# Filter turned in DRAM ahead of its stage, four staging places, and a new order of groups, closings and loads

## The chip, the cores and the metric

The kernel runs on one core of one Trainium2 chip. The metric is the device time of one execution in microseconds (us). Three executions of the kernel before took 1017.70, 1017.57 and 1022.55 us (median 1017.7). The profile comes from a further execution that took 1021.45 us; its span, from the first to the last instruction, is 1019.7 us, so 1.75 us lie around it.

## The reference, cut to what matters

S = 2048 rows, D = 576 columns, DFF = 4608, all float32.

```python
x  = A_q
xn = layernorm(x)
# A: short causal convolution of k (4 taps), times v, long causal convolution with ssm_k, gate
kv = sum(pad(k)[:, t:t + S] * shift_k[:, 3 - t] for t in range(4)) * v
y  = irfft(rfft(kv, 2 * S) * rfft(ssm_k.T, 2 * S))[:S] + kv * ssm_D      # per column, along S
A  = xn * y
# B: feed-forward
B  = relu(xn @ w1) @ w2                                                 # 576 -> 4608 -> 576
out = x + A + B
```

The filter `ssm_k` is stored as [D, S]: one row of 2048 values for each column d of the output.

## The kernel before, in words

Two things run interleaved, and TensorE (PE) works for both.

**The feed-forward** is the main line. It is cut into 36 steps ("quads"): two halves of the rows, each with 18 slices of 256 hidden units. The first three steps (`PLAIN`, up to about 95 us) use the plain product (`classical`), the other 33 a product with seven block products in place of eight (`quad`, L640). Weights and operands are split in a high and a low part, and three of the four part products are made. In a quad, PE makes the hidden values (`psh`, products of 512 columns) and between them eight "units" (`mm2`, L744) of the quad before: 12 products of 288 columns into one of two PSUM places (`pso`), whose sum VectorE (DVE) then adds to `acc` in SBUF (L772). A unit whose number is in `stage["seeded"]` goes another way: ScalarE (ACT) first copies `acc` into the PSUM place (L742), PE adds onto it, and ACT copies the result back to `acc` (L765); DVE has nothing to do for it. A quad's own DVE work is `sums` (L531), `u` (L697), `p` (L704), `ll` (L602); ACT makes the high parts (L518, L597), copies `psh` (L661, L699), and GpSimd (POOL) makes the low parts of the weights (L519) and issues the loads of the weights (`r<-in_w`, L500 to L511).

**The stream** `conv()` makes everything else and is a generator. `tick` (L1219) is called after each group of products with their column count; it pulls the next piece of the stream when its planned cost is covered. `yield` gives a cost, a negative number a pause in columns, and "wide" asks for a PSUM place borrowed from the units. `with here()` puts DVE and ACT instructions behind the feed-forward's last ones on the same engine. Each engine works its instructions in the order in which they were placed; a DMA has no such edge, and SP's queue is filled by the planner that lays out the program. The stages of the stream, with the times of the profiled execution, are:

1. `later_operands` (L401, 91 to 232 us). The second half of x is loaded (L408, `area<-in_x`), normalized, stored (`rows_n`, L428), loaded back in turned pieces (L444), transposed and combined into seven operands (L464). Each operand is split chunk by chunk, 14 chunks in all (n = 0 to 13): ACT makes the high part (L473) and DVE the low part (L474) in a staging place, and SP stores it (`ops<-area`, `ops_s<-area`, L476). There are three staging places, used in turn, so chunk n writes where chunk n - 3 was stored from.
2. The filter is loaded into `kt` by `load_filter` (L827): 16 DMAs of 288 KB, one for 36 columns d and one half of the SBUF partitions. With `d (p t) -> p d t`, t = 32, each piece of such a load is 32 values, 128 bytes. Eight of them are asked for beside the chunks from n = 6 on (L477), eight after them, each followed by a pause of `KT_GAP` = 6000 columns (L885 to L887).
3. The filter stage (L937 to L952, 262 to 338 us). 32 copies (L941, L943) bring `kt[:, :, t]` into order; 11 groups of products (`filter_group`, L903) each take up to 864 of 9216 columns, ACT and DVE copy the result from PSUM to `z` (L867, L869), and SP stores `z` to `zk` (L910), up to six stores a group. The last of the 11 groups is the short one (576 columns) and comes one copy after the tenth.
4. The input stage (338 to 650 us): taps, gate and products of k and v, stored to `zx`. Here units 3 and 4 of each quad are seeded (L955).
5. The middle stage (675 to 910 us): 18 pairs of chunks. For each, the filter's part is copied (L1044) and swapped (L1049), multiplied (L1074), swapped by four DMAs on SP (`area<-area`, L1079), joined by DVE (`join`, L1084), turned back on PE (`psg`/`psf`, L785) and stored to `zy`.
6. The output stage (910 to 999 us) loads `zy`, x and `fin` (L1150 to L1161), gates and adds.

`rate` (L1212) spreads the planned cost of the stream over the columns of the feed-forward that are left when all pauses are taken off.

Of the kernel before, what the change touches and what calls it, by code (L numbers as in the profile page):

```python
# [17 lines left out]
P = 128  # L18
# [18 lines left out]
A1 = 64  # L37
# [18 lines left out]
NCH = NG * D // CW  # L56
KG = 432
KD = 36
KT_GAP = 6000
N_FB, N_FS, N_FK, N_FX, N_FM, N_FO = 23, 14, A2, T * (2 * KS + 1) + 2, NCH // 2, T  # L60
W_FB, W_FS, W_FK, W_FX, W_FMK, W_FMX, W_FMB, W_FO = 2.6, 3.0, 1.9, 2.2, 4.0, 3.5, 2.9, 3.9
CONV_TOTAL = (N_FB * W_FB + N_FS * W_FS + N_FK * W_FK + N_FX * W_FX + N_FM * (W_FMK + W_FMX + W_FMB)
# [37 lines left out]
def h3_ffn_kernel(ctx: ExitStack, tc, x, k, v, shift_k, ssm_k, ssm_D, w1, w2, fwd, inv, mid, out):  # L100
# [26 lines left out]
    fin = dram.tile([HT // 2, P, 2, D], F32, name="fin")  # L127
    rows_n = dram.tile([HB, BT // 2, 2, P, D], F32, name="rows_n")
    ops_n = {o: dram.tile([P, 2, 2, 512], F32, name=f"ops_{o}") for o in OPERANDS}
    hl_n = dram.tile([HB, P, 512], F32, name="hl_n")  # L130
    scale_n = dram.tile([2 * BT, P], F32, name="scale_n")

# [27 lines left out]
    def halves(u):  # L160

        return slice(u * A1, (u + 1) * A1), slice((1 - u) * A1, (2 - u) * A1)

    def move(tile_, rows, t, store=False, queues=(nc.sync, nc.sync)):
        for u in range(U):
            a, b = tile_[halves(u)[0]], rows[u, :, t]
            queues[u].dma_start(*((b, a) if store else (a, b)))

    pairs = {}

# [146 lines left out]
    def spread_scales(pool):  # L317

        sq, turned = (pool.tile([P, 32], F32, tag=f"sq{n}", name=f"sq{n}") for n in range(2))
        nc.vector.tensor_copy(sq, rstd[:, :2 * BT].unsqueeze(1).to_broadcast([P, 4, 2 * BT]))  # L320
        nc.vector.transpose(turned, sq)
        for q in range(P // 32):
            queue = nc.scalar if q % 2 else nc.sync
            queue.dma_start(scale_n[:, 32 * q:32 * q + 32], turned[32 * q:32 * q + 2 * BT])
        for b in (1, 0):
            row[b] = pool.tile([P, 512], F32, tag=f"row{b}", name=f"row{b}")
            src = scale_n[b * BT:(b + 1) * BT].rearrange("(o i) p -> o (i p)", o=1)
            nc.sync.dma_start(row[b], src.to_broadcast([P, 512]))

    def scaled(o, b):  # L330
        if isinstance(o, int):
# [69 lines left out]
    def later_operands(view, views, load_filter):  # L401


        first = HB * BT
        rows = {}
        for t in range(first, T, 2):
            rows[t] = view((t - first) // 2 * 2 * D, 2, D)
            move(rows[t], x, slice(t, t + 2))  # L408
        yield -PAUSE
        for t0 in range(first, T, 4):  # L410
            for t in range(t0, t0 + 4):
                with here():
                    stats(t, rows[t - t % 2][:, t % 2, :])
                yield W_FB / 2
            shift = xp.tile([P, 4], F32, tag="shift", name=f"shift{t0}", bufs=2)
            with here():
                inv_std(t0, 4)
                nc.vector.scalar_tensor_tensor(shift, mv[:, t0:t0 + 4, 0], -1.0, rstd[:, t0:t0 + 4],
                                               op0=OP.mult, op1=OP.mult)
            yield W_FB / 2  # L420
            for t in range(t0, t0 + 4):
                pair = rows[t - t % 2]
                with here():
                    nc.scalar.activation(pair[:, t % 2, :], pair[:, t % 2, :], AF.Identity,
                                         scale=rstd[:, t:t + 1], bias=shift[:, t - t0:t - t0 + 1])
                yield W_FB / 2
                if t % 2:
                    nc.sync.dma_start(rows_n[t // BT - HB, t % BT // 2].rearrange("t p d -> p t d"),  # L428
                                      pair)
        order = [(b, c) for b in range(HB) for c in range(5)]  # L430
        yf = {f"{b}{k}": view(HB * BT * D + (2 * b + k) * 1024, 2, 512)
              for b in range(HB) for k in range(2)}
        for n, o in enumerate(("s1", "s2")):
            yf[o] = view(REST + 1024 * n, 2, 512)
        ws = {}

        def load(n):
            if n < len(order):
                b, c = order[n]
                src = rows_n[b].rearrange("h t (g p) d -> p (h t g) d", p=32)  # L440
                w = ws[n] = view(n % 4 * 512, 512)
                for i in range(4 if c < 4 else 2):
                    d = c * P + 32 * i
                    nc.sync.dma_start(w[32 * i:32 * i + 32].rearrange("p (g d) -> p g d", d=32),  # L444
                                      src[:, :, d:d + 32])

        for n in range(2):
            load(n)
        yield -PAUSE
        for n, (b, c) in enumerate(order):  # L450
            load(n + 2)
            with here():
                if c < 4:
                    nc.vector.transpose(yf[f"{b}{c // 2}"][:, c % 2, :], ws[n])
                else:
                    v, r = (view(2048 + (2 * b + k) * 512, 512) for k in range(2))
                    nc.vector.transpose(v[:64], ws[n][:64])
                    split_rest(r.bitcast(F32R), v)
                    nc.sync.dma_start(hl_n[b], r)
            yield W_FB  # L460
        n = 0
        stages_o = Ring(*views(REST + 2048, 2, 2, 512), view(3072, 2, 512))
        for o in ("00", "11", "s1", "s2", "01", "s3", "s4"):
            for c in range(2):  # L464
                with here():
                    combine(None, yf, (o,), c)
                if o[0] == "s":
                    yield W_FB / 2
                if n == HB * 3:
                    stages_o.views = (*stages_o.views[:2], yf["11"])  # L470
                dst = stages_o.put(n)
                with here():
                    nc.scalar.activation(dst[:, 0].bitcast(F32R), yf[o][:, c, :], AF.Copy)  # L473
                    nc.vector.tensor_tensor(dst[:, 1].bitcast(F32R), yf[o][:, c, :],  # L474
                                            dst[:, 0].bitcast(F32R), OP.subtract)
                nc.sync.dma_start(ops_n[o][:, :, c, :], dst)  # L476
                if n >= 6:  # L477
                    load_filter()
                n += 1
                yield W_FS  # L480
# [340 lines left out]
    def stages(view, views):  # L821


        kt = view(KT, NH, A2)
        blocks = [(d, h) for d in range(0, NH, KD) for h in range(2)]

        def load_filter():  # L827
            if blocks:
                d, h = blocks.pop(0)
                src = ssm_k[h * NH + d:h * NH + d + KD, :].rearrange("d (p t) -> p d t", t=A2)  # L830
                with here():
                    nc.sync.dma_start(kt[halves(h)[0], d:d + KD, :], src)

        z = view(Z, 2, 2 * CW)
        mats = Ring(*views(WT, 4, U, P))
# [62 lines left out]
                nc.vector.tensor_tensor(kt[row, :, 0], kt[row, :, 0], skip[row, :], OP.add)  # L898
        order = [T * u + t for t in range(T) for u in range(U)]
        flat = A2 * NH  # L900
        starts = list(range(0, flat, 2 * KG))

        def filter_group(a):  # L903
            parts = divided(a, min(a + 2 * KG, flat), KG, NH)
            group([[(w, lambda r, u=order[e] // T, t=order[e] % T: mats["k", t][:, u, :],
                     copies[e][:, c:c + w]) for e, c, w, _ in part] for part in parts],
                  KG, ("act", "dve"))
            for e, c, w, off in divided(a, min(a + 2 * KG, flat), flat, NH)[0]:
                for r in range(2):
                    nc.sync.dma_start(at_t(zk, order[e])[:, :, r * NH + c:r * NH + c + w],  # L910
                                      z[:, r, off:off + w])
# [25 lines left out]
        for e, t2 in enumerate(order):  # L937
            to = copies.put(e)
            with here():
                if e % 2:  # L940
                    nc.vector.tensor_copy(to, kt[:, :, t2])  # L941
                else:
                    nc.scalar.activation(to, kt[:, :, t2], AF.Copy)  # L943
            if e == A2 - 1:
                load(0)
            yield W_FK / 2
            while starts and min(starts[0] + 2 * KG, flat) <= e * NH + (e == A2 - 1) * NH:
                yield "wide"
                filter_group(starts.pop(0))
                yield W_FK / 2 / (len(range(0, flat, 2 * KG)) / A2)  # L950
            if e % U and e // U + 2 < T:
                load_mat(("k", e // U + 2), e // U + 2, nc.sync)  # L952


        stage["seeded"] = (3, 4)  # L955

        def tap(t, n):

# [110 lines left out]
        def multiplied(n, banks, filt):  # L1069

            for c in (1, 0):
# [4 lines left out]
                if c:  # L1076
                    for a in range(0, P, A2):
                        b = a ^ A2
                        nc.sync.dma_start(other[b:b + A2], filt[c][a:a + A2])  # L1079

        def join(n):
            to = parts[0][n]
# [98 lines left out]
                added.add(t)  # L1181

        for i in range(4):
            load_rest(i)
        for i in range(4):
            load_z(i)
        yield -1.75 * PAUSE
# [21 lines left out]

    stream = conv()  # L1210
    clock = {"ffn": 0.0, "conv": 0.0, "until": 1e9, "done": False, "wide": False}
    rate = CONV_TOTAL / (SHARE * FFN_TOTAL - PAUSES * PAUSE - 8 * KT_GAP)  # L1212

    def rest_of_stream():
        for _ in stream:
# [133 lines left out]
```

## Time and profile before

| | |
|---|---|
| three runs, median | 1017.70, 1017.57, 1022.55; 1017.7 us |
| profiled execution, its time | 1021.45 us |
| its span | 1019.7 us |
| granted PE clock over the span | 1.000 |
| PE, DVE, POOL, ACT busy | 99%, 68%, 45%, 43% of the span |

The profile names a group of instructions by line, engine and `out<-in`. A bracket such as `[2.19 <-ACT area L473]` is the idle time of the engine before the instruction, in us, and what ended it. `SPq` rows are DMA issues: the first number is when the issue began, the second how long SP was held; a DMA's landing is a different, later time. The view of waits has the total in us, the number of times, and the longest.

### The profile page before, as it was taken

What the parts mean: (1) busy time and instruction counts of PE and PEld (TensorE: products, weight loads), DVE (VectorE), ACT (ScalarE), POOL (GpSimd) and SP (SyncE); (2) the same over time, 40 slices, a digit from 0 to 9 for tenths busy, and PEclk for the clock granted to TensorE, in tenths of its full rate; (3) what the DMA queues carried; (4) which work ended last, traced back from release to release, by engine and by line L of the source; (5) the groups of instructions that cost most, each with busy time, mean ns of one, the idle gap of its engine ahead of it and who ended that gap; (6) DMA issues with size and microseconds to landing.
All of it is one profiled execution on the core that took longest, in us unless ns stands there. A gap on an engine that the chain in (4) does not pass through costs nothing.

```text
span 1019.7 us, 17381 instructions
## 1 busy us (share of the span) xinstructions
PE 1004.9 (99%) x6502; PEld 844.4 (83%) x6502; DVE 697.7 (68%) x1059; ACT 436.8 (43%) x765; POOL 460.5 (45%) x500
## 2 busy tenths in 40 slices
PE   9999999999999999999999999999999999999997
PEld 5998999889877898898889889887777777777787
DVE  6787677774665697787768768556667666666764
ACT  7244443443455244445354444544554544532220
POOL 4335444444443855645555454424533234434450
PEclk9999999999999999999999999999999999999999
DMA  6214389898465724359862433468889879878964
GB/s 172 90 50 113 102 186 193 186 224 137 135 204 183 214 76 129 93 167 376 255 193 89 136 107 91 153 184 241 247 242 262 269 230 276 222 220 240 277 183 116
DMA packets 129720, 185.22 MB, mean 182 GB/s; under 512 B 69042, under 2 KB 83508, under 8 KB 128740
## 3 DMA queue, kind: packets, MB, share of 16 engines
q1 hardware_dynamic: 113332, 130.82, 46.2%
q0 software_dynamic: 15952, 52.40, 17.4%
q8 instruction: 51, 0.84, 0.4%
q10 hardware_dynamic: 352, 0.89, 0.3%
q14 instruction: 33, 0.27, 0.1%
HBM read 119.57 MB, written 45.62 MB: 162 GB/s over the span
## 4 chain that ended last, share of the span: by engine, by line
PE 90%; DMA 4%; DVE 3%; issue 1%; ACT 1%; POOL 1%; SPq 0%; DVEq 0%; POOLq 0%; ACTq 0%
PE pso L575 42%; PE psh L575 34%; PE psg L785 5%; PE psf L785 4%; PE psh_c L575 3%; DMA ops_s<-area 1%; DMA r<-in_w 1%; DMA zk<-area 1%; PE psw L1260 1%; DVE ll L602 1%; DVE sums L531 0%; DVE x L297 0%; PE psx L235 0%; SPq L910 0%; POOL wd L519 0%
## 5 line engine op out<-in xcount | busy, mean ns | idle before, releaser
L575 PE MATMUL pso<-w,hh 128*128 128x288 f32 x2304 | 466.8, 296 | 1.0 <-DVE area L869 0.8
L575 PEld LDWEIGHTS pso<-w,hh 128*128 128x128 f32 x2304 | 378.0, 188 | 30.8 <-issue 7.6
L575 PE MATMUL pso<-w,ll 128*128 128x288 f32 x1152 | 339.5, 295 | 0.0
L772 DVE TENSOR_TENSOR acc<-pso,acc 128x576 f32<-128x576 f32 x240 | 180.4, 754 | 123.9 <-PE pso L575 123.3
L575 PEld LDWEIGHTS pso<-w,ll 128*128 128x128 f32 x1152 | 216.2, 188 | 0.0
L519 POOL TENSOR_TENSOR wb<-sums,wb 128x512 fp32r<-128x512 f32 x33 | 47.6, 1441 | 291.8 <-ACT wb L518 266.2
L519 POOL TENSOR_TENSOR w<-r,w 128x576 fp32r<-128x576 f32 x72 | 108.1, 1509 | 124.6 <-ACT w L518 124.4
L575 PE MATMUL psh<-x,wa 128*128 128x512 f32 x396 | 102.4, 394 | 3.3 <-DVE p L704 2.2
L575 PE MATMUL psh<-xs,wb 128*128 128x512 f32 x396 | 102.1, 393 | 0.0
L575 PEld LDWEIGHTS psh<-x,wa 128*128 128x128 f32 x396 | 72.4, 188 | 18.8 <-DVE p L704 2.7
L575 PE MATMUL psh<-hl,wr 128*128 128x512 f32 x264 | 85.3, 404 | 0.8 <-ACT psh L699 0.8
L602 DVE SCALAR_TENSOR_TENSOR ll<-psh,hh 128x512 fp32r<-128x512 f32 x66 | 45.3, 687 | 55.1 <-ACT hh L597 55.1
L519 POOL TENSOR_TENSOR wa<-r,wa 128x512 fp32r<-128x512 f32 x36 | 56.5, 1570 | 54.0 <-ACT wa L518 53.9
L575 PEld LDWEIGHTS psh<-xs,wb 128*128 128x128 f32 x396 | 70.8, 188 | 11.4
L699 ACT ACTIVATE psh<-psh 128x512 f32<-128x512 f32 x33 | 19.2, 582 | 117.4 <-DVE u L697 117.4
L785 PE MATMUL psg<-area 64*64 64x512 f32 (+10 forms) x632 | 64.2, 472 | 1.5 <-issue 1.5
L575 PEld LDWEIGHTS psh<-hl,wr 128*128 128x128 f32 x264 | 45.9, 188 | 21.6 <-issue 10.8
L597 ACT ACTIVATE hh<-psh 128x512 fp32r<-128x512 f32 x66 | 39.3, 595 | 47.6 <-PE psh L575 47.4
L597 ACT ACTIVATE hh<-p 128x512 fp32r<-128x512 f32 x33 | 20.9, 634 | 88.1 <-PE pso L575 43.4
L697 DVE TENSOR_TENSOR u<-psh,u 128x512 f32<-128x512 f32 x33 | 22.8, 691 | 45.3 <-PE psh L575 45.2
L785 PE MATMUL psf<-area 64*64 64x512 f32 (+10 forms) x528 | 51.1, 451 | 0.7 <-DVE area L941 0.7
L575 PE MATMUL psh<-xs,wc 128*128 128x512 f32 x198 | 51.2, 393 | 0.0
(137 smaller groups left out, 1498.9 us busy)
## 6 DMA issues: line engine op xcount, KB each, us to landing
r<-in_w POOLq DMA_DIRECT2D x70, 288.0 KB, 4.0
area<-area SPq DMA_DIRECT2D x144, 128.0 KB, 4.8
r<-in_w POOLq DMA_DIRECT2D x35, 512.0 KB, 4.9
zk<-area SPq DMA_DIRECT2D x64, 144.0 KB, 2.9
area<-zk SPq DMA_DIRECT2D x18, 512.0 KB, 4.3
area<-zx SPq DMA_DIRECT2D x18, 512.0 KB, 6.2
zy<-area SPq DMA_DIRECT2D x18, 512.0 KB, 3.1
area<-zy SPq DMA_DIRECT2D x32, 288.0 KB, 7.2
```

The costliest lines, as they stand in the source:

```text
L519: nc.gpsimd.tensor_tensor(w[:, 1, :n], src, w[:, 0, :n], OP.subtract)
L575: last = nc.tensor.matmul(ps, a, m, start=start and n == 0, stop=n == len(seq) - 1, skip_group_check=True)
L597: done["act"] = nc.scalar.activation(hh, ps, AF.Relu)
L602: done["ll"] = nc.vector.scalar_tensor_tensor(ll, ps, 0.0, hh, op0=OP.max, op1=OP.subtract)
L697: nc.vector.tensor_tensor(u2, x, u2, OP.add)
L699: nc.scalar.activation(x, y, AF.Copy, scale=-1.0)
L772: done["acc"] = nc.vector.tensor_tensor(two(acc[t]), ps[:, :, :NH], two(acc[t]), OP.add)
L785: done["pe"] = nc.tensor.matmul(ps, a, m, start=start, stop=stop, skip_group_check=True)
L1260: last = nc.tensor.matmul(idle[0], warm[:, :P], warm, start=True, stop=True)
```

## The change

- `relay_filter` is new. It copies `ssm_k` to a DRAM tensor `kt_n` [half, p, d, t] by 16 DRAM-to-DRAM DMAs, 288 KB each, with the same 128-byte pieces. Ten of them stand on SP behind the loads of the scales (`row`, L328, in `spread_scales`), six behind the loads of the second half of x.
- `load_filter` loads from `kt_n`: 8 DMAs of 576 KB on all 128 partitions, 4608 bytes in one piece for each partition. Four are asked for beside the chunks n = 6, 8, 10 and 12, four after them, each with a pause of 9000 columns. `rate` subtracts 4 x 9000 in place of 8 x 6000.
- The staging of the chunks has three places for n = 0 to 5 and four for n = 6 to 13 (the fourth is where operand "s1" was, no longer needed then).
- The 11 filter groups are cut so that the first is the one with 576 columns. A group is made as soon as its columns are copied, so the groups now follow copies 2, 5, 8, ..., 29 and 31 in place of 3, 6, ..., 30 and 31 (counted from 0).
- In the input stage units 3 and 7 are seeded in place of 3 and 4.
- At the start of the output stage the first four `load_rest` (x on SP, `inv` on POOL) have an edge behind the last swap of the middle stage (L1079).

```diff
-KT_GAP = 6000
+KT_GAP = 9000
+FIRST = 5 * KD
...
+    kt_n = dram.tile([U, A1, NH, A2], F32, name="kt_n")
...
+    def relay_filter(behind, part):
+        for d in range(*part, KD):
+            for h in range(U):
+                src = ssm_k[h * NH + d:h * NH + d + KD, :].rearrange("d (p t) -> p d t", t=A2)
+                with tc.issue_after(behind.ins):
+                    behind = nc.sync.dma_start(kt_n[h, :, d:d + KD, :], src)
...
-            nc.sync.dma_start(row[b], src.to_broadcast([P, 512]))
+            last = nc.sync.dma_start(row[b], src.to_broadcast([P, 512]))
+        relay_filter(last, (0, FIRST))
...
-            move(rows[t], x, slice(t, t + 2))
+            last = move(rows[t], x, slice(t, t + 2))
+        relay_filter(last, (FIRST, NH))
...
-        stages_o = Ring(*views(REST + 2048, 2, 2, 512), view(3072, 2, 512))
+        two_o = views(REST + 2048, 2, 2, 512)
+        stages_o = [*two_o, view(3072, 2, 512)] * 2 + [*two_o, yf["11"], yf["s1"]] * 2
...
-                if n == HB * 3:
-                    stages_o.views = (*stages_o.views[:2], yf["11"])
-                dst = stages_o.put(n)
+                dst = stages_o[n]
...
-                if n >= 6:
+                if n >= 6 and n % 2 == 0:
                     load_filter()
...
-        blocks = [(d, h) for d in range(0, NH, KD) for h in range(2)]
+        blocks = list(range(0, NH, KD))
...
-                d, h = blocks.pop(0)
-                src = ssm_k[h * NH + d:h * NH + d + KD, :].rearrange("d (p t) -> p d t", t=A2)
+                d = blocks.pop(0)
                 with here():
-                    nc.sync.dma_start(kt[halves(h)[0], d:d + KD, :], src)
+                    nc.sync.dma_start(kt[:, d:d + KD, :],
+                                      kt_n.rearrange("h p d t -> (h p) d t")[:, d:d + KD, :])
...
-        starts = list(range(0, flat, 2 * KG))
+        cuts = [0, *range(flat % (2 * KG), flat + 1, 2 * KG)]
+        spans = list(zip(cuts, cuts[1:]))
...
-            while starts and min(starts[0] + 2 * KG, flat) <= e * NH + (e == A2 - 1) * NH:
+            while spans and spans[0][1] <= e * NH + (e == A2 - 1) * NH:
                 yield "wide"
-                filter_group(starts.pop(0))
+                filter_group(*spans.pop(0))
...
-        stage["seeded"] = (3, 4)
+        stage["seeded"] = (3, 7)
...
-                        nc.sync.dma_start(other[b:b + A2], filt[c][a:a + A2])
+                        done["swap"] = nc.sync.dma_start(other[b:b + A2], filt[c][a:a + A2])
...
         for i in range(4):
-            load_rest(i)
+            with tc.issue_after(done["swap"].ins):
+                load_rest(i)
...
-    rate = CONV_TOTAL / (SHARE * FFN_TOTAL - PAUSES * PAUSE - 8 * KT_GAP)
+    rate = CONV_TOTAL / (SHARE * FFN_TOTAL - PAUSES * PAUSE - 4 * KT_GAP)
```

More of the change, by code (lines that the diff above doesn't have):

```diff
@@ L166, in move @@
             a, b = tile_[halves(u)[0]], rows[u, :, t]
-            queues[u].dma_start(*((b, a) if store else (a, b)))
+            last = queues[u].dma_start(*((b, a) if store else (a, b)))
+        return last
     pairs = {}
@@ L900, in stages, with filter_group @@
         flat = A2 * NH
-        starts = list(range(0, flat, 2 * KG))
-        def filter_group(a):
-            parts = divided(a, min(a + 2 * KG, flat), KG, NH)
+        cuts = [0, *range(flat % (2 * KG), flat + 1, 2 * KG)]
+        spans = list(zip(cuts, cuts[1:]))
+        def filter_group(a, b):
+            parts = divided(a, b, KG, NH)
             group([[(w, lambda r, u=order[e] // T, t=order[e] % T: mats["k", t][:, u, :],
@@ L907, in filter_group @@
                   KG, ("act", "dve"))
-            for e, c, w, off in divided(a, min(a + 2 * KG, flat), flat, NH)[0]:
+            for e, c, w, off in divided(a, b, flat, NH)[0]:
                 for r in range(2):
@@ L946, in stages @@
             yield W_FK / 2
-            while starts and min(starts[0] + 2 * KG, flat) <= e * NH + (e == A2 - 1) * NH:
+            while spans and spans[0][1] <= e * NH + (e == A2 - 1) * NH:
                 yield "wide"
-                filter_group(starts.pop(0))
-                yield W_FK / 2 / (len(range(0, flat, 2 * KG)) / A2)
+                filter_group(*spans.pop(0))
+                yield W_FK / 2 / ((len(cuts) - 1) / A2)
             if e % U and e // U + 2 < T:
                 load_mat(("k", e // U + 2), e // U + 2, nc.sync)
-        stage["seeded"] = (3, 4)
+        stage["seeded"] = (3, 7)
         def tap(t, n):
```

## The prediction

> **What bounds the kernel now.** I read the page's head first, then the waits of PE alone, then the chain that ended last, and then the timeline around each wait.
>
> ```profile
> span 1019.7 us, 17381 instructions
> PE 1004.9 (99%) x6502; PEld 844.4 (83%) x6502; DVE 697.7 (68%) x1059; ACT 436.8 (43%) x765; POOL 460.5 (45%) x500
> ```
>
> PE is busy for 1004.9 of 1019.7 us, and no other engine is near; the granted clock is 1.00 in every window below. The change neither removes nor adds a product, so all it can win is idle time of PE: 14.8 us. Part of that is the start and the last store. The view of PE's waits between 40 and 1000 us shows the rest (who waited for whom: us in total, times, longest):
>
> ```profile
> PE psh L575 <- DVE p L704: 2.2, 1, 2.2
> PE psg L785 <- issue: 1.5, 1, 1.5
> PE psh L575 <- ACT psh L661: 1.0, 1, 1.0
> PE pso L575 <- DVE area L869: 0.8, 1, 0.8
> PE psh L575 <- ACT psh L699: 0.8, 1, 0.8
> PE psf L785 <- DVE area L941: 0.7, 1, 0.7
> PE pso L575 <- DVE acc L772: 0.2, 1, 0.2
> ```
>
> These seven single waits add up to 7.2 us; that is the ceiling. Since ends of products are modelled, I check the largest pair by the distance of equal steps, in the chain (start, length, what):
>
> ```profile
> 143.80 3.23 PE psh L575 x14
> ...
> 168.06 3.23 PE psh L575 x14
> ...
> 193.76 7.79 DMA ops_s<-area
> ...
> 220.40 3.23 PE psh L575 x14
> ```
>
> A quad without stream products takes 168.06 - 143.80 = 24.26 us. From 168.06 to 220.40 stand two: 52.34 - 48.52 = 3.82 us lost, where the waits on L704 and L661 show 3.2. The chain says by what: stores of operand chunks.
>
> **The staging places.** Picked from the timelines of ACT, DVE and PE there (start, length, instruction, idle time before it and what ended it):
>
> ```profile
> 201.63 0.63 ACT L473 ACTIVATE area<-area 128x512 fp32r<-128x512 f32 x1 [2.66 <-DMA ops_s<-area]
> 202.30 0.69 DVE L474 TENSOR_TENSOR area<-area 128x512 fp32r<-128x512 f32 x1 [2.60 <-ACT area L473]
> 204.91 1.65 PE L575 MATMUL psh<-x,wa 128*128 128x512 f32 x6 [2.23 <-DVE p L704]
> 207.64 0.63 ACT L473 ACTIVATE area<-area 128x512 fp32r<-128x512 f32 x1 [0.92 <-DMA ops_s<-area]
> ```
>
> ACT stands 2.66 us because its staging place is still being stored. DVE works in order, so L704, which PE needs, stands behind L474. The store issued at 193.76 had landed only at 201.55. Why so late (a stretch with each engine's busy time, clock, DMA share and GB/s; the issues of the filter loads, ns, and their landing; the speed in 40 slices of 222 to 232 us):
>
> ```profile
> 160.00:240.00 80.00, 76.75 (x460) 69.36 (x459) 55.44 (x83) 33.58 (x63) 37.38 (x38) 1.00 1.00 209
> L832 SPq DMA_DIRECT2D area<-in_ssm_k x16: 613/1616/4447, 161.1 to 233.1; - x16
> DMA to landing us min/median/max: 4.7/6.2/11.3
> GB/s 192 264 120 150 92 387 252 340 461 457 426 422 391 356 329 222 224 218 208 172 118 75 161 167 184 153 147 143 140 135 147 157 145 141 143 147 143 141 139 153
> ```
>
> From 160 to 240 us the DMA engines are busy all the time (share 1.00). In the last row the speed is 329 to 461 GB/s while a chunk is stored, but about 143 where only filter loads run. One filter load of 288 KB (294,912 bytes) thus takes 2.1 us of all 16 engines, sixteen 33 us of these 80.
>
> The change takes all sixteen out of this stretch and puts eight loads of 576 KB there, in pieces of 4608 bytes. For these I take the mean speed of the row at 160 to 240 us, 209 GB/s, as the slow bound (2.8 us each, 23 us) and 461 as the fast one (1.3 us, 10 us). I use the middle, 16 us: the stretch falls from 80 to some 63 us of DMA work. A store then lands about two thirds as late, and the fourth place lets it land one chunk later, 6.0 us by the two rows of L473. The waits of 2.66 and 0.92 us need that margin only once. **I take 3.8 us off**; bounds are 0 and 3.8. The last loads still come behind chunk 13, since they overwrite its sources. With four pauses of 9000 columns in place of eight of 6000, the filter stage begins 12,000 columns earlier, 5.4 us by 3.23 us for 14 x 512. Its planned end is the same (`rate` falls by 0.8%), so I count no time for it.
>
> **The relay.** Its 16 DMAs go to SP, behind these rows of SP's queue:
>
> ```profile
> 33.97 0.82 SPq L328 DMA_DIRECT2D row<-scale_n  x2
> 91.62 4.95 SPq L167 DMA_DIRECT2D area<-in_x  x8
> 124.11 2.94 SPq L428 DMA_DIRECT2D rows_n<-area  x2
> 34.00:91.00 57.00, 56.90 (x335) 51.19 (x334) 44.78 (x64) 21.27 (x41) 24.57 (x27) 1.00 0.21 66
> ```
>
> SP issues nothing between 34.8 and 91.6 us, and nothing from 96.6 to 124.1. Ten relays fit in the first gap (57 us, DMA share 0.21) and six in the second (27 us). No row shows a DRAM-to-DRAM copy. The nearest is the filter load itself, with the same pieces and the same source: 2.1 us each. If reading and writing do not overlap, twice that. I take 2.5: 25 us and 15 us, both hidden. SP is held as long (1.6 us each in the median row of L832), with nothing behind. The weight loads on POOL's queue share the engines, but at 160 to 240 us they do so with a share of 1.00, and no PE wait names them there. The price is 0 unless a relay takes over 57/10 = 5.7 us; that is a rival below.
>
> **The filter groups.** Picked from the timelines of SP (issue, time held) and DVE:
>
> ```profile
> 316.33 13.33 SPq L910 DMA_DIRECT2D zk<-area  x11
> 329.77 0.61 DVE L869 COPY area<-psf 128x432 f32<-128x432 f32 x1 [4.07 <-DMA zk<-area]
> 336.37 0.61 DVE L869 COPY area<-psf 128x432 f32<-128x432 f32 x1 [3.88 <-DMA zk<-area]
> ```
>
> SP spends 13.33/11 = 1.2 us on a store and falls behind; a group's copies wait until `z` has been stored, and the two last groups, one copy apart, wait 4 us each. PE's waits of 0.8 (L869) and 0.7 (L941) follow. With the short group first, two stores fewer stand before every later group (4 + 6(i - 2) before group i in place of 6(i - 1)), worth 2.4 us. The tenth comes after copy 29 in place of 30, the last still after 31. So the waits of 4 us shrink to about 1.6, where PE lost 0.8: **1.5 us off**. If this saves nothing, 0.
>
> **The loads of the output stage.** Picked from the timelines of SP, DVE and PE:
>
> ```profile
> 887.60 5.80 SPq L167 DMA_DIRECT2D area<-in_x  x5
> 895.97 2.59 SPq L1079 DMA_DIRECT2D area<-area  x4
> 892.42 1.72 DVE L1084 SCALAR_TENSOR_TENSOR area<-area,sign 128x1024 f32<-128x1024 f32 x1 [3.31 <-DMA area<-in_x]
> 904.34 1.28 DVE L1084 SCALAR_TENSOR_TENSOR area<-area,sign 128x1024 f32<-128x1024 f32 x1 [0.80 <-DMA area<-area]
> 905.72 1.09 PE L785 MATMUL psg<-area 64*64 64x512 f32 x8 [1.50 <-issue]
> ```
>
> The x loads come between the last two swaps. The join before the last waits 3.31 us, everything after it is late, and the last join ends at 905.62, 0.1 us before PE's late `psg`. Behind the last swap, the x loads no longer stand there. The last join waits for its swap still, but both are up to 3.3 us earlier: **1.5 us off**. Eight loads then hold SP for 8 x 1.16 = 9.3 us from about 895; the first output products come only after a pause of 28,000 columns (12.6 us), so they stay hidden.
>
> **Seeded units 3 and 7.** Twice 24/2 = 12 quads (x24 below):
>
> ```profile
> L742 ACT ACTIVATE pso<-acc x24: 656/657/680, 356.7 to 645.1; 128x576 f32<-128x576 f32 x24
> 469.96 0.76 DVE L772 TENSOR_TENSOR acc<-pso,acc 128x576 f32<-128x576 f32 x1 [0.82 <-PE pso L575]
> 471.35 0.63 PE L575 MATMUL psh<-hl,wr 128*128 128x512 f32 x2
> ```
>
> Work stays equal: one unit in each quad moves from ACT to DVE, one from DVE to ACT. Unit 7's copy must wait for unit 5's DVE add. That ends at 470.72, the copy takes 0.66, and PE has `psh` to do until 471.98: 0.6 us to spare. Where DVE is later than that, each quad loses up to 0.6. In exchange DVE has less at the end of the quad, where L699's wait (0.8) arose. Bounds: -1.0 (with the 0.2) and +7.2 (12 x 0.6); I take 0, as no wait of PE in this stage comes from a copy L742 now. The queue behind such a copy on ACT is the high part of the hidden values (L597), which the quad after needs.
>
> **The sum.** 1021.45 - 3.8 - 1.5 - 1.5 = 1014.65, say **1014.6 us**. That is against the profiled execution's own time, which is 3.75 above the median. The runs lie at two levels, 1017.6 and 1022. If the lower ones already lack part of these waits, the changed kernel's median stays at 1014.6; if they save elsewhere, it is 1017.7 - 6.8 = 1010.9.
>
> **Rivals.** *The runs at 1017.6 have the waits too:* 1010.9. For it: one profile cannot tell the two levels apart, and the start before 40 us hangs on loads too. Against: the largest wait itself hangs on a landing, which is what differs from run to run.
> *A new wait eats the gain:* closings at unit 7 cost 0.3 us in 12 quads, or the staging wait goes only by half: 1014.6 + 3.6 = 1018.2. For it: DVE is busy for 68% of the span and works in order. Against it: only one wait of PE, 0.8 us, lies in the stage with the closings now.
>
> *The relay overruns (slower):* at the longest landing seen, 11.3 us (filter loads: 4.7/6.2/11.3), ten relays in turn end at 34.8 + 113 = 148. The x loads of 91.62 queue behind them, the statistics on DVE wait with them, and DVE's in-order adds stop PE: about 56 less the pause of 16,000 columns (7.2 us), 49 us, for 1063. It decides from 5.7 us a relay on; each further us costs 10, after the first 7.2. Against it: 2.1 us for the same pieces into SBUF.
> The Trainium skill, "DMA: Bandwidth & Descriptors", Specifications, speaks for this rival: below 512 bytes a transfer is no longer at line rate and is done as a read-modify-write. The fall from 461 to 143 GB/s agrees in direction, but on loads; no run here shows such writes to DRAM.
>
> **How the numbers follow.** Forecast 0.50 (own range 1013 to 1016.5); runs with the same waits 0.25 (1009.5 to 1012.5); new wait 0.17 (1016.5 to 1021); relay 0.08 (over 1023). The range 1010.0 to 1019.5 leaves out the relay and the ends of the others, 0.18 in all. A measurement of this kernel tells about 0.5% from no change, here 1012.6 and 1022.8. Faster: 0.25 and 0.05 of the forecast's lower end, 0.30. Slower: 0.08 and 0.01, 0.09. Same: 0.61.
>
> **What would show it.** Right: no wait of ACT on `ops_s<-area`, a distance of 48.5 us for two quads there, the relays landed before 91 us, DVE's waits on `zk<-area` under 2 us, no idle PE before the last `psg`. Wrong: relays of over 5.7 us; L742 waits that end in PE waits on `pso`; new PE waits elsewhere, as the stream now meets other places of the quads.

## The result, and the profile after

The changed kernel took 1013.73 us in the median of six runs (1013.15 to 1014.29), the kernel before 1017.74 us beside it (1017.54 to 1022.55). The ratio is 0.9948 with a 95% interval of 0.9934 to 0.9962; it is formed from the runs and isn't the quotient of the two medians, which is 0.9961. The runs after lie within 1.1 us, those of before within 5. One run of the kernel l5 below took 5500 us at a granted clock of 0.167 and is in no ratio. The profiled execution took 1014.12 us, 7.33 less than the 1021.45 before.

The head of the page and the waits of PE from 40 to 1000 us (who waited for whom: us in total, times, longest), after:

```profile
span 1012.3 us, 17374 instructions
PE 1004.2 (99%) x6502; PEld 844.8 (83%) x6502; DVE 683.6 (68%) x1057; ACT 438.1 (43%) x769; POOL 444.8 (44%) x500
```

```profile
PE pso L586 <- DVE acc L783: 0.4, 1, 0.4
```

Of seven waits with 7.2 us one is left, with 0.4. Where the time came from is read from the windows. A row has the stretch, its length, the busy times of PE, PEld (weight loads of PE), DVE, ACT and POOL, then granted clock, DMA share and GB/s; the difference between length and PE's busy time is what PE idles. Before:

```profile
40.00:240.00 200.00, 196.66 (x1172) 177.96 (x1171) 145.70 (x239) 83.39 (x156) 94.16 (x97) 1.00 0.66 148
240.00:350.00 110.00, 108.48 (x877) 90.23 (x876) 65.80 (x109) 48.71 (x94) 49.52 (x61) 1.00 0.60 177
350.00:650.00 300.00, 299.04 (x1929) 263.40 (x1928) 228.86 (x311) 137.90 (x246) 159.75 (x157) 1.00 0.50 156
880.00:910.00 30.00, 28.50 (x179) 22.82 (x178) 17.81 (x27) 12.45 (x21) 10.55 (x14) 1.00 0.80 228
```

and after:

```profile
40.00:240.00 200.00, 199.90 (x1193) 181.34 (x1192) 148.20 (x241) 84.60 (x158) 98.31 (x100) 1.00 0.67 175
160.00:240.00 80.00, 80.00 (x482) 72.81 (x481) 58.67 (x86) 34.78 (x65) 41.91 (x42) 1.00 0.66 221
240.00:350.00 110.00, 110.00 (x890) 92.14 (x890) 69.54 (x114) 51.79 (x98) 50.56 (x64) 1.00 0.55 172
350.00:650.00 300.00, 300.00 (x1950) 264.17 (x1952) 213.67 (x313) 135.57 (x245) 139.11 (x153) 1.00 0.50 158
880.00:910.00 30.00, 29.50 (x186) 23.37 (x180) 15.65 (x24) 11.64 (x20) 11.82 (x13) 1.00 0.87 264
```

PE gains 3.24 us in the stage of the operands, 1.52 in the filter stage, 0.96 in the input stage and 1.00 at the seam to the output stage. That is 6.7; the other 0.7 is PE's own busy time, 1004.9 before and 1004.2 after. From 160 to 240 us the DMA share fell from 1.00 to 0.66, and the stores of the 14 chunks land sooner. Before (issues at L476) and after (L487):

```profile
DMA to landing us min/median/max: 5.5/6.1/7.8
```

```profile
DMA to landing us min/median/max: 3.0/3.0/7.3
```

The relay and the two quads that lost 3.82 us before, from the timeline of SP (start, time held, issue), the group of the new loads (ns: shortest, median, longest), and the chain that ended last:

```profile
35.39 22.49 SPq L171 DMA_DIRECT2D kt_n<-in_ssm_k  x10
92.31 5.69 SPq L176 DMA_DIRECT2D area<-in_x  x8
98.04 18.62 SPq L171 DMA_DIRECT2D kt_n<-in_ssm_k  x6
```

```profile
L842 SPq DMA_DIRECT2D area<-kt_n x8: 320/384/677, 162.4 to 220.6; - x8
```

```profile
168.79 3.23 PE psh L586 x14
...
217.31 3.23 PE psh L586 x14
```

A relay holds SP for 22.49/10 = 2.25 us in the first gap and 3.1 in the second; the first ten are issued by 57.9 us, well before the loads of x at 92.31. The two quads take 217.31 - 168.79 = 48.52 us, which is twice 24.26: nothing is lost there.

### The profile page after: what moved, and what is told of

It reads as the page before. It is cut to its first block, busy times and chain, and to the rows that moved or that the text cites. A ratio compares the mean times of both kernels' runs of the same rounds, so it can differ in the third digit from the quotient of the medians.

```text
span 1012.3 us, 17374 instructions
## 1 busy us (share of the span) xinstructions
PE 1004.2 (99%) x6502; PEld 844.8 (83%) x6502; DVE 683.6 (68%) x1057; ACT 438.1 (43%) x769; POOL 444.8 (44%) x500
## 4 chain that ended last, share of the span: by engine, by line
PE 98%; ACT 1%; DVE 0%; issue 0%; ACTq 0%
PE pso L586 45%; PE psh L586 38%; PE psg L796 5%; PE psf L796 5%; PE psh_c L586 3%; PE psw L1273 1%; ACT x L304 0%; DVE x L307 0%; DVE acc L783 0%; PE psx L245 0%; ACT w L529 0%; ACT wb L529 0%; ACT xf L316 0%; ACT xs L224 0%; ACT hh L608 0%
## 5 line engine op out<-in xcount | busy, mean ns | idle before, releaser
L530 POOL TENSOR_TENSOR wa<-r,wa 128x512 fp32r<-128x512 f32 x36 | 48.5, 1347 | 52.5 <-ACT wa L529 52.4
L1086 DVE TENSOR_TENSOR area<-psf,area 128x512 f32<-128x512 f32 x72 | 44.7, 683 | 11.5 <-PE psf L796 9.4
L586 PE MATMUL psh<-x,wc 128*128 128x512 f32 x198 | 51.2, 394 | 0.0
```

Source lines behind the costliest of these rows:

```text
L530: nc.gpsimd.tensor_tensor(w[:, 1, :n], src, w[:, 0, :n], OP.subtract)
L586: last = nc.tensor.matmul(ps, a, m, start=start and n == 0, stop=n == len(seq) - 1, skip_group_check=True)
L1086: nc.vector.tensor_tensor(filt[c][:, k, :], banks[k], filt[c][:, k, :], OP.mult)
```

## The experiments

Line numbers from L171 on are those of the changed kernel, unless a kernel is built from the one before. The medians, and the ratios to the kernel before that ran beside each (its medians there were 1018.7 to 1019.0):

| run | median us | ratio, 95% interval |
|---|---|---|
| the change | 1013.73 | 0.9948 (0.9934 to 0.9962) |
| u1, without the relay | 1016.21 | 0.9973 (0.9962 to 0.9985) |
| u2, three places | 1013.88 | 0.9949 (0.9936 to 0.9963) |
| s, four places alone | 1017.61 | 0.9985 (0.9976 to 0.9993) |
| r3, thirty relays | 1019.99 | 1.0010 (1.0001 to 1.0018) |
| u5, x loads without the edge | 1015.85 | 0.9968 (0.9956 to 0.9979) |
| u4, units 3 and 4 seeded | 1013.62 | 0.9949 (0.9937 to 0.9961) |
| u3, short group last | 1020.67 | 1.0021 (1.0011 to 1.0030) |
| s, short group first alone | 1020.39 | 1.0013 (1.0005 to 1.0022) |
| a, pauses of 12,000 | 1024.10 | 1.0057 (1.0044 to 1.0069) |
| u3, short last, pauses of 12,000 | 1023.46 | 1.0044 (1.0032 to 1.0056) |
| f8, pauses of 8000 | 1024.92 | 1.0054 (1.0040 to 1.0068) |
| l5, short last, pauses of 5000 | 1018.69 | 1.0006 (0.9991 to 1.0022) |

### Staging places or the crowd of filter loads

u1, the changed kernel without the relay; each of the eight filter steps loads its two halves from `ssm_k`, in 128-byte pieces:

```diff
-        relay_filter(last, (0, FIRST))
...
-        relay_filter(last, (FIRST, NH))
...
-                    nc.sync.dma_start(kt[:, d:d + KD, :],
-                                      kt_n.rearrange("h p d t -> (h p) d t")[:, d:d + KD, :])
+                    for h in range(2):
+                        src = ssm_k[h * NH + d:h * NH + d + KD, :].rearrange("d (p t) -> p d t", t=A2)
+                        nc.sync.dma_start(kt[halves(h)[0], d:d + KD, :], src)
```

> The changed kernel with the relay left out: the filter is loaded into SBUF in 128-byte pieces as before (two loads of 288 KB for each block of 36 columns), with four staging places and the new pauses. If the crowded DMA stretch is what made the staging wait (my theory), stores land late again and four places cover only a part: the wait of ACT on ops_s<-area returns or DVE's p comes late, PE idle 0.5 to 3 us between 175 and 235 us, 1014.5 to 1017 us. Rival, the number of places alone decides: no wait, 1013.7 within 0.5.

u2, the changed kernel with three places again:

```diff
-        stages_o = [*two_o, view(3072, 2, 512)] * 2 + [*two_o, yf["11"], yf["s1"]] * 2
+        stages_o = [*two_o, view(3072, 2, 512)] * 2 + [*two_o, yf["11"]] * 3
```

> The changed kernel with three staging places from n = 6 on, as before; the relay stays. If the crowded DMA stretch is the cause, a store lands within some 5 us and three places are enough: no idle PE there, 1013.7 within 0.7. Rival, the number of places decides: ACT waits on ops_s<-area as before, PE loses 2 to 3.8 us, 1015.7 to 1017.5 us.

And the kernel before with the four places of the change, and nothing else of it:

> The kernel before with four staging places for the chunks 6 to 13 and nothing else. Theory of the crowd (the stores land late because sixteen filter loads of 128-byte pieces hold the DMA engines; the fourth place only hides a part): DMA share of 0.95 or more from 160 to 240 us, 1 to 2.5 us less than the kernel before beside it, a wait of ACT on ops_s<-area of 0.5 to 2 us left. Theory of the places (three places are too few, whatever the loads): no wait of ACT on ops_s<-area, 3 us or more less than the kernel before beside it.

The windows of u1 and of the four places alone, in this order:

```profile
160.00:240.00 80.00, 78.78 (x473) 71.21 (x472) 56.63 (x85) 34.44 (x65) 39.64 (x40) 1.00 1.01 219
```

```profile
160.00:240.00 80.00, 78.81 (x475) 71.66 (x474) 55.32 (x85) 34.53 (x65) 40.29 (x39) 1.00 1.00 215
```

Both have the fourth place, both have the 128-byte loads in this stretch, and both keep a DMA share of 1.00 or 1.01 and lose 1.2 us of PE there, where before lost 3.25. ACT's waits on `ops_s<-area` tell the same; the rows are those of u1, of the four places alone, and of u2:

```profile
ACT area L482 <- DMA ops_s<-area: 1.9, 1, 1.9
```

```profile
ACT area L472 <- DMA ops_s<-area: 1.8, 1, 1.8
```

```profile
ACT area L484 <- DMA ops_s<-area: 1.8, 1, 1.8
```

Before it was 3.6 us in two waits. The places alone are worth 0.0015 x 1019 = 1.5 us (0.7 to 2.4). Taking the relay from the change costs 2.5 us; 1.2 of them are PE's idle time in this stretch, the rest lies elsewhere. Taking the fourth place from it costs 0.15, within the runs' spread: with the relay ACT waits 1.8 us once, much as in the other two, but PE does not wait behind it. What made the stores late was the crowd; the fourth place covered part of it and is no longer needed.

### How much cover the relay has

r3, the changed kernel with twenty more copies ahead of the first ten, into two tensors that nobody reads:

```diff
+    idle_n = [dram.tile([U, A1, NH, A2], F32, name=f"idle_n{i}") for i in range(2)]
...
-        relay_filter(last, (0, FIRST))
+        for to in (*idle_n, kt_n):
+            last = relay_filter(last, (0, FIRST), to)
```

> The changed kernel with 20 more copies of the filter, of the same pieces, into two DRAM tensors that nobody reads, ahead of the first ten relays: thirty in the gap of SP that held ten. At 2.25 us each they hold SP until about 103 us, where the loads of the second half of x begin at 92.3 us now. Theory of the threshold (the relay costs nothing only as long as it fits into the gap): the loads of x begin 9 to 13 us later, statistics on DVE wait for them, PE idles 3 to 10 us between 95 and 125 us, 1017 to 1024 us. Theory that there is cover left behind the gap: the loads of x are as late, but PE idles no more than 1 us there, 1013 to 1015 us.

SP's timeline, and the windows of the gap and of the stretch behind the loss in it (granted clock third from the end):

```profile
34.54 44.63 SPq L173 DMA_DIRECT2D idle_n<-in_ssm_k  x20
79.22 21.18 SPq L173 DMA_DIRECT2D kt_n<-in_ssm_k  x10
100.51 6.97 SPq L179 DMA_DIRECT2D area<-in_x  x8
```

```profile
34.00:92.00 58.00, 53.92 (x307) 48.06 (x306) 41.55 (x60) 19.18 (x37) 22.15 (x24) 0.97 1.01 182
87.00:89.20 2.20, 2.20 (x10) 2.10 (x10) 0.00 (x0) 0.58 (x1) 2.20 (x3) 0.50 1.00 159
```

The loads of x begin 8.2 us later than in the changed kernel, a little under the 9 to 13 expected, and PE is busy for all of 103 to 130 us: no wait of PE comes from them. The time is in the first theory's range all the same. Most of the 6.3 us are lost ahead of these loads: PE idles 4.1 us between 34 and 92, and behind that the granted clock falls to 0.50 (second row). Another 0.9 us is idle time of PE between 650 and 880 us. PE's row at the first loss, and ACT's (the bracket is the idle time before and what ended it):

```profile
84.11 0.73 PE L590 MATMUL psh<-x,wa 128*128 128x512 f32 x2 [3.34 <-ACT wa L533]
```

```profile
80.87 0.60 ACT L612 ACTIVATE hh<-psh_c 128x512 fp32r<-128x512 f32 x1 [2.66 <-PE psh_c L590]
...
83.45 0.61 ACT L533 ACTIVATE wa<-r 128x512 fp32r<-128x512 f32 x1
```

The high part of the first quad's weights (`wa`) stands behind this `hh` and the copies `xs`, `hl` and `x` on ACT; in the changed kernel it ran at 79.08, ahead of all of them. Its load was issued at 59.13 us, and the loads of that line land within 4.7; ACT idled 2.66 us ahead of this run of work. So ACT's order made `wa` late, not a transfer. The thirty relays came with another layout of the program, and its order on ACT cost the time.

The loss also moved what needs the loads. The statistics of these rows on DVE begin at 115.05 us in the changed kernel, and here at:

```profile
119.92 1.53 DVE L193 BATCH_NORM_STATS2 bn<-area 128x6 f32<-128x288 f32 x4
```

They are 4.9 us later, so the loads begin only 8.2 - 4.9 = 3.3 us later against the work that reads them. This run shows cover of at least 3.3 us behind the gap. It doesn't reach the 7.2 us of the pause, and doesn't show what a slower relay alone would cost.

### The loads of the output stage, and the closings

u5 takes the edge behind the last swap away from the first four `load_rest`:

```diff
-            with tc.issue_after(done["swap"].ins):
-                load_rest(i)
+            load_rest(i)
```

> The changed kernel without the edge that puts the x and inv loads of the output stage behind the last swap. My theory: the x loads stand between the last swaps again, the join before the last waits about 3 us and PE waits 1.5 us before the last psg: 1015.2 (1014.5 to 1016). Rival, chance meeting: 1013.7 within 0.5.

The wait came back, by the view of PE's waits:

```profile
PE psg L796 <- issue: 1.4, 1, 1.4
```

The time is 2.1 us over the change. In its profile 1.3 of them stand at this seam (PE busy 28.18 of the 30 us from 880 to 910, 29.50 in the changed kernel); the rest lies elsewhere, as an edit in one place also moves the waits of others. u4 seeds units 3 and 4 again (`stage["seeded"] = (3, 4)`):

> The changed kernel with units 3 and 4 seeded as before. My theory: the closings neither cost nor win, 1013.7 within 0.6. Rival: with unit 4 in place of 7 DVE is late at the end of a quad (p, ll), small PE waits return in the input stage, 1014.5 to 1017 us.

1013.62 against 1013.73, with the same single wait of 0.4 us: which units are seeded makes no difference here. The 0.96 us from 350 to 650 us is thus not theirs; no run separated which edit it came from.

### The filter groups

u3, the changed kernel with the short group last; its counterpart is the kernel before with the short group first and nothing else (the same two lines the other way round):

```diff
-        cuts = [0, *range(flat % (2 * KG), flat + 1, 2 * KG)]
+        cuts = [*range(0, flat, 2 * KG), flat]
```

> The changed kernel with the short filter group last again. If two stores fewer before each group and the wider last gap removed the waits (my theory), PE's waits on the copies of the last two groups return, 0.8 + 0.7 us: about 1015.2 (1014.5 to 1016). Rival, the waits before were a chance meeting of the groups with the quads, gone because the stage now starts 5.4 us earlier: 1013.7 within 0.5.

> The kernel before with the short filter group first and nothing else. If the group order is worth its two waits: 0.8 + 0.7 us less than the kernel before beside it, 1.5 us (0.8 to 2.5). If order and start act together: anything from no gain to a loss of 5 us.

Undoing the order costs about 7 us, far more than expected; making it alone gains nothing (1.3 us slower). So the order cannot be worth a fixed sum. Next the start of the stage was put back to where it stood before, with either order, by `KT_GAP` = 12,000:

> The changed kernel with pauses of 12000 columns after the last four filter loads, so the filter stage starts where it did before. If the order of the groups removes the waits wherever the stage meets the quads: no PE wait between 255 and 350 us, 1013.7 within 0.7. If the start of the stage decides (its end meets the weight loads on POOL's queue), PE waits appear there: 1015 to 1019 us.

> The changed kernel with the short group last and pauses of 12000 columns: group order and start of the filter stage both as before. With the short group last and the early start the time was 1020.7. If the order alone costs that, this gives 1020.7 within 1. If order and start act together, the stage loses what it lost before the change, 0.8 + 0.7 us: about 1015.3 (1014.5 to 1016.5).

Both lose about 10 us, whichever group is first, more than any of the theories on record had. A theory was then formed on the distance between the last two groups, and tested with pauses of 8000 (short group first) and of 5000 (short group last):

> The changed kernel with pauses of 8000 columns in place of 9000; the short filter group stays first, and no store and no wait is added. By the order of the program the last two filter groups then stand 3.7 us of products apart, where they stand 10.0 us apart with 9000. Theory of the meeting (what counts is how close the last filter groups fall behind each other between the quads' products, since each waits for the stores of the one before): PE waits of 4 to 8 us in all that hang on zk<-area, 1017 to 1022 us, the last two groups about 5 us apart. Theory of the order (the short group first is what saves): the same time as the changed kernel, 1013 to 1015 us, PE waits under 1.5 us.

> The changed kernel with the short filter group last again and pauses of 5000 columns, so that by the order of the program the last two groups stand 6.2 us of products apart and the weight loads stand ahead of the k and v loads on POOL's queue. Theory of the meeting: PE waits of 0 to 2 us, 1013 to 1016 us, although the short group is last. Theory of the order: as with the short group last and pauses of 9000, 1018.5 to 1022 us, PE waits of 4 us and more.

f8 is slow, as that theory had it and beyond its range, but no wait of PE there hangs on `zk`. l5 is 5 us over the change, against it (its profiled execution took 1022.22, 3.5 above its median, so its waits are not set against its time). The distance of the last groups isn't the cause either. What f8, the pauses of 12,000 and u3 share is seen in the chain that ended last. Of f8, of the pauses of 12,000, and of u3:

```profile
322.50 7.87 DMA area<-in_shift_k
...
330.94 0.78 POOL r L511
...
332.77 1.29 POOL wc L530
...
334.10 1.29 PE psh L586 x4
335.39 2.88 PE pso L586 x12
```

```profile
329.81 8.90 DMA zk<-area
...
...
339.49 3.25 PE pso L586 x12
```

```profile
329.80 8.80 DMA r<-in_w
...
338.69 6.19 DVE sums L542 x3
```

Each has a transfer that is issued between 322 and 330 us and takes 8 to 9 us. For f8 that is only part of the account: from 310 to 350 us PE idles 2.6 us and runs a while at half clock, and it loses about as much again at the seam to the output stage, where it idles 2.96 us before the last `psg` and the clock falls once more:

```profile
898.00:901.00 3.00, 2.77 (x11) 1.19 (x12) 0.13 (x1) 0.65 (x1) 0.00 (x0) 0.54 1.04 252
```

The median landing of all `zk` stores of the changed kernel is 2.5 us and that of its weight loads (`r<-in_w`) 4.3. What crowds the engines then are the first loads of the input stage, k, v and the taps, on POOL's queue. The changed kernel has the same crowd (windows), but what PE needs next is out of it (DVE's, POOL's and ACT's timelines, and then ACT's of u3):

```profile
325.00:330.00 5.00, 5.00 (x49) 4.22 (x42) 3.59 (x6) 3.21 (x6) 4.47 (x8) 1.00 0.99 227
330.00:335.00 5.00, 5.00 (x32) 4.58 (x31) 0.91 (x2) 1.98 (x4) 3.13 (x7) 1.00 1.05 374
```

```profile
325.27 0.61 DVE L880 COPY area<-psf 128x432 f32<-128x432 f32 x1 [0.98 <-PE psf L796]
```

```profile
326.16 1.31 POOL L530 TENSOR_TENSOR wc<-sums,wc 128x512 fp32r<-128x512 f32 x1
```

```profile
332.53 0.60 ACT L693 ACTIVATE p<-psh 128x512 f32<-128x512 f32 x1
335.96 0.63 ACT L529 ACTIVATE wa<-r 128x512 fp32r<-128x512 f32 x1 [2.83 <-DMA r<-in_w]
```

```profile
338.68 0.63 ACT L529 ACTIVATE wa<-r 128x512 fp32r<-128x512 f32 x1 [7.23 <-DMA r<-in_w]
339.22 0.58 ACT L693 ACTIVATE p<-psh 128x512 f32<-128x512 f32 x1
```

Its last group's copy waits for no store. The low part of the weights (`wc`) is made at 326.16, ahead of the weight loads, where f8 makes it at 332.77, behind them. The transfers are slow here as well: the weight load takes 7.9 us to land, u3's 8.8, and the last six `zk` stores 8.0 to 9.7. But the copy `p`, which PE needs, stands ahead of `wa` on ACT, and in u3 behind it: there ACT waits 7.23 us for the weight load, and PE idles 2.65 us behind `p`. So it is the meeting of the filter stage's end, the quad's weights and these loads that decides, and the order and the pauses together set it. This reading was formed after the runs; no run moved the k and v loads alone, so as a cause it is argued from the traces of four kernels, not shown by an undoing.

## Why the prediction was right, and where it was not

The forecast was 1014.6 us against the profiled execution, which took 1014.12; the median is 1013.73. That the changed runs stay where their profile is, and did not come out at 1010.9, fits the reading that the lower runs of before lacked part of the waits. But there are no two levels: 29 more runs of the kernel before, beside f8, l5, r3 and the four places alone, spread from 1016.85 to 1021.53 us without a gap. The profiled execution stood at the upper end of that spread, so of the 6.8 us summed up from its waits the medians show 4.0. The sum itself came out partly by luck: the windows show 3.24 us for the 3.8 and 1.00 for the 1.5 of the output stage, and the 0.96 of the input stage and 0.7 less busy time, which weren't in the sum, made up for it.

**The staging places, -3.8.** Right in mechanism, and near in size: the windows show 3.24. The places alone bring 2.06 of it (PE busy 78.81 in place of 76.75 us), the relay the rest; by the medians they are worth 1.5 and 2.5, but those hold gains and losses elsewhere too. The DMA work was to fall to 63 of 80 us; it fell to a share of 0.66, 53 us. The split between the two was not foreseen: with the relay the fourth place is worth 0.15 us.

**The relay, 0.** Right: 2.25 us a copy in the first gap against 2.5 taken, and no PE wait. Its threshold stays untested: in r3 the x loads were 8.2 us late by the clock, but 3.3 against the work that reads them, less than the 7.2 us of the pause. The thirty relays lost their time mostly by another way, the place of `wa` on ACT.

**The filter groups, -1.5.** The sum came out (1.52 us in the window), the reason did not: this is the step that failed. It held that two stores fewer ahead of each group shorten the waits, whatever else moves. With the order alone nothing was gained. The waits on `zk` were to be under 2 us and are not (DVE's waits in the changed kernel: total, times, longest; before it was 15.9, 8, 4.1):

```profile
DVE area L880 <- DMA zk<-area: 11.0, 7, 3.3
```

PE no longer pays for them because of where they fall. The pauses were costed at nothing, since the planned end stays the same; with 8000 or 12,000 in place of 9000 the time is over 10 us longer, in f8 nearly half of it at the seam to the output stage. The 1.5 was right by luck, by a good meeting of these.

**The loads of the output stage, -1.5.** Right: without the edge PE waits 1.4 us again, and the median is 2.1 us longer. **The closings, 0.** Right: 0.1 us, within the spread. Neither bound, -1.0 nor +7.2, was touched.

**The rivals.** The new wait that eats the gain (1018.2) did not come in the changed kernel, but in six of its neighbours it did (r3 and the five with another order or other pauses), at 1018.7 to 1024.9 us; the chance of 0.17 for it was rather low. For the overrun of the relay, the Trainium skill, "DMA: Bandwidth & Descriptors", Specifications, spoke of a read-modify-write below 512 bytes. Here 288 KB in 128-byte pieces took 2.25 us written to DRAM and 2.1 us written to SBUF before, so no run shows a price of writing on top of it.

## What to carry to other kernels

Where a store lands late, look first at what shares the DMA engines with it: loads in small pieces, moved to a stretch where SP and the engines are free, were worth more than another buffer. Undo each part of a change and also shift it in time: what parts cost by undoing, from nothing to 7 us, doesn't add up to the total of 4 to 5, since each edit moves the waits of other stages too. When a run delays something, measure it against the work that needs the data, not by the clock. When a stage's start or order is moved, read who issues transfers at its seam to the next stage, and keep what the bounding engine needs ahead of them on each queue.

## What was not expected of the hardware

A wait of PE can cost nearly twice its length. Two waits of PE, of l5 and of f8:

```profile
PE psh L586 <- POOL wr L530: 1.8, 1, 1.8
```

```profile
PE psh L586 <- POOL wc L530: 2.3, 1, 2.3
```

These are windows of before, behind its wait of 2.23 us, and of l5 and f8, behind these two:

```profile
204.80:207.00 2.20, 2.09 (x11) 1.83 (x12) 1.32 (x3) 1.77 (x4) 0.80 (x1) 1.00 1.01 344
```

```profile
331.00:334.00 3.00, 3.00 (x14) 2.90 (x14) 0.91 (x2) 1.08 (x2) 2.98 (x5) 0.50 0.29 76
```

```profile
336.00:338.00 2.00, 2.00 (x10) 2.00 (x9) 0.00 (x0) 1.12 (x2) 1.98 (x4) 0.50 0.72 196
```

The granted clock stayed at 1.00 in before, after the longer idle, and fell to 0.50 after 1.8 us in l5. In f8, 12 products of `pso` that take 1.59 us at full clock took 2.88 (the chain above), so with the products on either side its idle of 2.3 us cost about 1.8 more. The length of the idle stretch thus doesn't decide alone. In all kernels here, between 40 and 1010 us, no idle stretch of 0.9 to 1.7 us was followed by a lower clock, and each of the six of 2.3 us or more was (f8 2.3 and 3.0, u3 2.7, r3 3.3, the two with pauses of 12,000 4.7 and 4.8); between them 1.8 was and 2.23 was not. The Trainium skill, "TensorE: Matmul & The Clock Gate", Part 1, tells of a gate that looks at activity in windows of 3.4 us that run freely, and grants half the clock after an idle one. The halves agree with the 0.50, and free-running windows would explain why 2.23 us cost nothing where 1.8 did; no run here shows the windows themselves. But these idle stretches were shorter than a whole window, so less than a whole idle one is enough here.
